# Retention and a Swish MLP in one program: wider transfers for half of w_in, its up projections in groups of four, and later scores for the first two tails

## The chip, the cores and the metric

The kernel runs on one core of one Trainium2 chip. The metric is device time in microseconds (us). A core has TensorE (PE; its weight loads are listed apart as PEld), VectorE (DVE), ScalarE (ACT), GpSimd (POOL) and SyncE (SP), which issues nearly all transfers of this kernel. PE writes into PSUM, here eight banks of 128 x 512 f32 values; DVE and ACT copy from there into the on-chip memory SBUF.

## What is computed

Retention over 8 batches, 8 heads, 576 positions and 64 values a head, and behind it an MLP with a Swish whose beta differs by column:

```python
scores = scale * np.matmul(q, k.transpose(0, 1, 3, 2))
Dmat = np.where(rel >= 0, gamma[:, None, None] ** rel[None, :, :], 0.0)
attn_out = np.matmul(scores * Dmat, v)
x = attn_out.transpose(0, 2, 1, 3).reshape(B * S, H * D)    # 4608 x 512
h = x @ w_in                                                # w_in: 512 x 2048
g = h * (1.0 / (1.0 + np.exp(-beta * h)))
out = g @ w_out                                             # w_out: 2048 x 512
```

## The kernel before

**Tiles.** Of each batch's 576 positions, 512 are four chunks of 128 (`seq` entries 0 to 31); the last 64 positions are its tail. Two batches' tails make one chunk of 128, so there are four tails (entries 32 to 35). The MLP works on blocks of 512 rows: block m is batch m's chunks, and block 8 is the four tails together. The blocks' order is 0 to 6, 8, 7 (L49).

**MLP.** For a block, `up` (L480) makes one of 16 tiles of 128 columns of h by four matmuls of 128x512 (one for each `ko`, a quarter of the 512 inputs) into a PSUM bank; ACT takes the Swish of it into `gT`. `down` (L514) adds four matmuls at a time into an accumulator `po`; after 16 it is copied to `ot` and sent out. Block 0's first six tiles of h are made in pairs by `up_pair` (L493): u = 0 does the first two `ko` of both, u = 1 the last two.

**Weights.** `pieces` (L165) cuts w_in into eight pieces of 256 columns. `load_w_in` (L171) brings a piece in with rows of 1 KB, the first three pieces in two halves by `ko`; two pieces share one tile `wt`, of which there are four. `cast_w_in` (L180) makes bf16 of it, four casts of 128x256 for a piece, even `ko` on POOL and odd on DVE. `load_w_out` (L189) reuses the `wt` tiles, in rows of 2 KB, and `cast_w_out` (L195) scales and casts. All loads of w_in are issued before the first matmul of the program, w_out's in the list below, and behind these the loads of the next batches.

**Retention.** For a batch, POOL (DVE at first) scales q and casts k (`kn`, L288), v is scaled (`vn`, L268); PE or, from batch 2 on, a transposing transfer (L296) turns them. A tail takes six loads (L108), POOL's preparation `pre` (L276 to L278) and one transposing transfer, `x_tail`. `first(i)` (L654) makes the scores of entries i and i + 1 (`a_sc`, L328): 8 matmuls each into two banks, the even entry's with the tag "sc" and the odd one's with "O"; DVE multiplies them with the causal mask into `R`. `tails(i)` (L674) makes the outputs of two tails (`a_O4` L442, `a_cross4` L459) in the two "O" banks, which `x4` (L470) copies, one by ACT and one by DVE. A tail's tile `tln` shares the tag "qn", of two buffers, with the tiles of q.

**Order.** The kernel writes its order out by hand. `fill` is a list of PE's large units (one `up`, or four matmuls of `down`: 0.86 us each). Streams of other steps have positions in that list; `merged` (L541) runs a step ahead of the first unit whose number is not below its position, and steps of equal position in the order of their streams. So each engine, SP's queue too, does its part in this order. `base[n]` is the number of the first unit of the n-th block. The tails hang on block 6: with its first unit as 0, the loop at L703 puts `first` of batch 7's chunks at 3 and 10, of tails 32 and 33 at 17, and of tails 34 and 35 at 24; `tails` comes 5 later. `pair_prep` (L680) puts the loads, preparations and transposes at fixed distances ahead of `first`. Around the first two tails the list before is, with numbers counted from block 6's first unit:

```
-14 load_tail(0)  -4.5 pre(32)  -4 load_tail(1)  -3 x_k(7, 1)  -3 load_tail(2)
4 pre(33)  4 load_tail(3)  5 x_tail(32)  6.5 pre(34)  7.5 x_tail(33)
12 pre(35)  12 x_tail(34)  14.5 x_tail(35)  15 outputs(28)
17 first(32)  22 tails(32)  24 first(34)  29 tails(34)  32 up(8, 0)
```

PSUM's eight banks are three of tag "mm" (`ph`, `po`), two "O", two "sc" and one "st".

Of the kernel before, what the change touches and what calls it, by code (L numbers as in the profile page):

```python
# [11 lines left out]
F32 = mybir.dt.float32  # L12
# [7 lines left out]
def kernel(  # L20
# [11 lines left out]
    B, H, S, D = q.shape  # L32
    d_model = H * D
    d_ff = moe_w_in.shape[1]
    N = B * S
    P = 128
    HP = H // 2
    KO = d_model // P
    FO = d_ff // P
    MB = 512  # L40
# [21 lines left out]
    psum = ctx.enter_context(tc.psum_pool(name="psum", bufs=1))  # L62
# [68 lines left out]
    for h in range(H):  # L131
# [15 lines left out]
                            fill=0.0, base=0, channel_multiplier=-1)  # L147
# [14 lines left out]
    tiny = consts.tile([P, FO], F32, name="tiny")  # L162
    WG = 4

    pieces = [(f, 256) for f in range(0, d_ff, 256)]  # L165
    NP = len(pieces)
    w_in_r = moe_w_in.rearrange("(ko ki) f -> ki ko f", ki=P)
    w_out_r = moe_w_out.rearrange("(fo fi) n -> fi fo n", fi=P)
    wts, whole = {}, [None]

    def load_w_in(g):  # L171
        f0, fn = pieces[g]
        if f0 % 512 == 0:
            whole[0] = stage.tile([P, KO, 512], F32, name="wt", tag="wt", bufs=4)
        t = whole[0][:, :, f0 % 512:f0 % 512 + fn]
        for w in (slice(0, 2), slice(2, KO)) if g < 3 else (slice(0, KO),):
            nc.sync.dma_start(t[:, w], w_in_r[:, w, f0:f0 + fn])  # L177
        wts[g] = t

    def cast_w_in(g, kos=range(KO)):  # L180
        t = wts[g]
        f0, fn = pieces[g]
        for ko in kos:
            if ko % 2 == 0:
                nc.gpsimd.tensor_copy(w_in_sb[:, ko, f0:f0 + fn], t[:, ko])  # L185
                continue
            nc.vector.tensor_copy(w_in_sb[:, ko, f0:f0 + fn], t[:, ko])  # L187
# [16 lines left out]
    for g in range(NP):  # L204
        load_w_in(g)
# [284 lines left out]

    phs = {}

    def up_pair(m, fo, u):  # L493

        if m not in gts:
            gts[m] = sb.tile([P, FO, CB, P], BF16, name="gT", tag="gT", bufs=2)
        fs = (fo, fo + 1)
        if u == 0:
            tag = ("mm", "O", "sc")[fo // 2]
            for f in fs:  # L500
                phs[f] = psum.tile([P, MB], F32, name="ph", tag=tag, bufs=3 if tag == "mm" else 2)
        for ko, f in [(ko, f) for ko in (2 * u, 2 * u + 1) for f in fs]:
            nc.tensor.matmul(phs[f][:], w_in_sb[:, ko, f * P:(f + 1) * P], xts[m][:, ko],
                             start=(ko == 0), stop=(ko == KO - 1))
            if ko == KO - 1:
                nc.scalar.activation(gts[m][:, f], phs[f][:], ACT.Silu, scale=beta_sb[:, f:f + 1])
# [44 lines left out]
    def F(f, *a):  # L551
        return lambda: f(*a)
# [5 lines left out]
    for n in range(4):  # L558
# [34 lines left out]
    a_cross(3, True)  # L593
    a_O(3)
    cast_w_in(0, (0, 1))
    a_x(3)
    cast_w_in(0, (2, 3))
    a_st(3)
    cast_w_in(1)
    nc.vector.reciprocal(rbeta_sb[:], beta_sb[:])  # L600

    nc.gpsimd.memset(causal2[:], 1.0)
    nc.gpsimd.affine_select(out=causal2[:], in_=causal2[:], pattern=[[1, P]], compare_op=ALU.is_ge,
                            fill=0.0, base=0, channel_multiplier=-1)
    nc.gpsimd.memset(causal2[:TL, TL:], 0.0)

    fill = [F(up_pair, 0, fo, u) for fo in (0, 2, 4) for u in range(2)] + [F(up, 0, fo) for fo in range(6, FO)]
    d0 = len(fill)
    def down_rows(n):

# [69 lines left out]
    def pair_prep(i, at):  # L680
        b, c = seq[i]
        if b is None:
            if c:
                return [(at - 27, F(load_tail, c)), (at - 20, F(load_tail, c + 1)), (at - 17.5, F(pre, i)),
                        (at - 12, F(pre, i + 1)), (at - 12, F(x_tail, i)), (at - 9.5, F(x_tail, i + 1))]
            return [(at - 31, F(load_tail, c)), (at - 21.5, F(pre, i)), (at - 21, F(load_tail, c + 1)),
                    (at - 13, F(pre, i + 1)), (at - 12, F(x_tail, i)), (at - 9.5, F(x_tail, i + 1))]
        n, st = full.index(i), []
        if b == XB:
            if c == 0:  # L690
                return [(d0 + 13, F(pre, i + x, (0,))) for x in range(2)] + \
                       [(d0 + 14, F(pre, i + x, (1,))) for x in range(2)]
            return [(u1 + 8 + x / 2, F(pre, i + x)) for x in range(2)]
        if c == 0:
            st += [(at - 30, F(load_q, b, (0,)))] + ([(at - 30, F(x_k, XB, 1))] if b == XB + 1 else [])
            st += [(at - 30, F(load_q, b, (1,)))] + [(at - 20 + x, F(pre_q, b, x)) for x in range(4)]
            st += [(at - 14 + 1.5 * x, F(x_q, b, x)) for x in range(2)]
        early = b == XB + 1 and c > 0
        return st + [(at - (25.4 if early else 28), F(load_kv, n)), (at - (25.3 if early else 26), F(load_kv, n + 1)), (at - 16, F(pre, i)),
                     (at - 15, F(pre, i + 1)), (at - (13 if c else 11.5), F(x_k, b, c // 2))]  # L700

    todo = list(range(2 * CB, len(seq), 2))
    for n in range(1, B - 1):  # L703

        take = [i for i in todo if seq[i][0] == n + 1 or n == B - 2]
        todo = todo[len(take):]
        lo, hi = (base[n] + 17, base[n + 1] - 9.5) if n == 1 else (base[n] + 3, base[n + 1] - 8)
        at = [lo + x * (hi - lo) / (len(take) - 1) for x in range(len(take))]
        if len(take) == 2 and n > 1:
            at[1] -= 6  # L710
        for i, t in zip(take, at):
            st = pair_prep(i, t) + [(t, F(first, i))]
            if seq[i][0] is None:
                st.append((t + 5, F(tails, i)))
            elif seq[i][1] > 0:
                st.append((t + 5, F(outputs, i - 2)))
            streams.append(st)
# [32 lines left out]
```

## Time and profile before

| What | Value |
|---|---|
| Median of three runs | 304.92 us (304.61 to 305.0) |
| The profiled execution | 304.39 us |
| Its span (first to last instruction) | 302.7 us |
| PE busy in the span | 296.1 us |
| ACT / POOL / DVE busy | 133.8 / 108.2 / 103.8 us |
| 128x512 matmuls of up (L487) and of down (L521) | 592 and 608, the costliest groups of PE |
| Granted PE clock | 1.0 all the way |

The span is what the profile covers; 1.7 us of the execution's time lies around it. A line of a timeline gives start and length in us, engine, line of the kernel, operation, what is written and read, how many instructions were merged and, in brackets, the idle time of the engine before it and who ended that. SPq is SP issuing transfers. In the table of stretches, each engine has its busy us and its number of instructions in brackets; PE's clock, the share of the 16 DMA engines and GB/s follow.

### The profile page before, as it was taken

To read this page: it belongs to the slowest core of one execution; us is meant where nothing else is said; L and a number is where in the kernel's file an instruction comes from. 1 tells how busy PE (TensorE), PEld (TensorE's weight loads), DVE (VectorE), ACT (ScalarE), POOL (GpSimd) and SP (SyncE) were. 2 spreads that over 40 slices of the span, in tenths; PEclk is the share of its full clock that TensorE was granted. 3 is DMA by queue.
4 is the path that set the end of the run, shared out by engine and by line. 5 is a ranking of instruction groups with operands and counts; after the bars stand their busy time and mean duration, and the time that the engine had idled before them with its cause. 6 is when DMAs were issued, how large, how long until landed. Compare 5 with 4: busy or idle time off the path is not lost.

```text
span 302.7 us, 5782 instructions
## 1 busy us (share of the span) xinstructions
PE 296.1 (98%) x2345; PEld 151.5 (50%) x2345; DVE 103.8 (34%) x192; ACT 133.8 (44%) x227; POOL 108.2 (36%) x212
## 2 busy tenths in 40 slices
PE   8799999999999999999999999999999999999996
PEld 5554455855544454445444544454454444444444
DVE  6554556604640443043222413151346510020012
ACT  5577446781247223732274227521761058107700
POOL 3666007673942733551355043960452000000000
PEclk9999999999999999999999999999999999999999
DMA  8999999999999999909991899997996100131011
GB/s 212 220 346 364 383 253 241 221 193 241 180 243 272 254 199 225 260 13 167 248 244 37 158 229 248 212 184 186 193 196 108 70 36 0 36 70 35 2 69 69
DMA packets 129290, 53.86 MB, mean 178 GB/s; under 512 B 110048, under 2 KB 122736, under 8 KB 129264
## 3 DMA queue, kind: packets, MB, share of 16 engines
q1 hardware_dynamic: 129232, 53.49, 80.0%
q8 instruction: 18, 0.29, 0.4%
q14 instruction: 8, 0.07, 0.1%
q10 hardware_dynamic: 32, 0.01, 0.0%
HBM read 36.71 MB, written 9.44 MB: 152 GB/s over the span
## 4 chain that ended last, share of the span: by engine, by line
PE 84%; DMA 8%; SPq 5%; POOL 1%; issue 0%; DVE 0%
PE po L521 38%; PE ph L487 37%; DMA kvn<-in_k_dram 3%; SPq L94 3%; PE sc L338 3%; DMA wt<-in_moe_w_out_dram 3%; PE O L455 2%; DMA wt<-in_moe_w_in_dram 2%; PE st L413 2%; PE O L467 1%; SPq L82 1%; SPq L177 1%; POOL w_in_sb L185 0%; PE O L386 0%; PE T L318 0%
## 5 line engine op out<-in xcount | busy, mean ns | idle before, releaser
L489 ACT ACTIVATE gT<-ph,beta_sb 128x512 bf16<-128x512 f32 (+1 forms) x148 | 97.0, 659 | 80.8 <-PE ph L487 80.6
L521 PE MATMUL po<-w_out_sb,gT 128*128 128x512 bf16 (+2 forms) x608 | 129.1, 368 | 0.0
L487 PE MATMUL ph<-xT,w_in_sb 128*128 128x512 bf16 (+1 forms) x592 | 122.8, 365 | 0.0
L521 PEld LDWEIGHTS <-gT 128*128 128x128 bf16 x608 | 56.9, 98 | 63.4
L487 PEld LDWEIGHTS <-w_in_sb 128*128 128x128 bf16 x592 | 56.8, 98 | 60.7 <-POOL w_in_sb L185 0.7
L343 DVE TENSOR_TENSOR R<-sc,causal 128x512 bf16<-128x512 f32 x72 | 45.0, 684 | 79.1 <-PE sc L338 79.0
L528 DVE COPY ot<-po 128x512 f32<-128x512 f32 (+2 forms) x34 | 22.4, 658 | 77.2 <-PE po L521 77.2
L288 POOL CAST kn<-kvn 128x128 bf16<-128x128 f32 (+2 forms) x80 | 25.8, 357 | 59.7 <-DMA kvn<-in_k_dram 59.3
L268 POOL TENSOR_TENSOR vn<-kvn,gv 128x512 bf16<-128x512 f32 x32 | 33.3, 1042 | 8.7 <-DMA kvn<-in_v_dram 4.8
L257 POOL TENSOR_TENSOR qs<-qn,gq 128x256 bf16<-128x256 f32 (+1 forms) x36 | 26.3, 758 | 27.6 <-DMA qn<-in_q_dram 27.6
L421 ACT CAST sbq<-st 128x256 bf16<-128x256 f32 x18 | 6.7, 371 | 35.8 <-PE st L413 35.8
L475 DVE CAST xT<-O 128x512 bf16<-128x512 f32 x20 | 12.7, 685 | 20.9 <-PE O L467 20.9
L338 PE MATMUL sc<-qT,kT 64*128 64x128 bf16 x256 | 10.8, 218 | 0.6 <-ACT kT L319 0.6
L338 PEld LDWEIGHTS <-kT 64*128 64x128 bf16 x288 | 8.2, 94 | 5.5 <-issue 3.8
L475 ACT CAST xT<-O 128x512 bf16<-128x512 f32 x8 | 4.7, 589 | 13.4 <-PE O L467 13.4
L276 POOL TENSOR_TENSOR kn<-tln,gq 128x128 bf16<-128x128 f32 (+1 forms) x12 | 5.6, 470 | 13.6 <-DMA tln<-in_q_dram 7.1
L185 POOL CAST w_in_sb<-wt 128x256 bf16<-128x256 f32 x16 | 7.2, 472 | 5.4 <-DMA wt<-in_moe_w_in_dram 5.2
L210 PE MATMUL ph<-warm 128*128 128x128 f32 (+1 forms) x24 | 7.3, 444 | 1.2 <-DVE warm L119 1.2
L455 PE MATMUL O<-R,vn 128*64 128x128 bf16 x224 | 7.7, 220 | 0.0
L187 DVE CAST w_in_sb<-wt 128x256 bf16<-128x256 f32 x16 | 5.3, 360 | 6.6 <-DMA wt<-in_moe_w_in_dram 6.6
L413 PEld LDWEIGHTS <-kn 128*64 128x64 bf16 x192 | 4.8, 111 | 5.5 <-issue 4.2
L202 DVE TENSOR_SCALAR w_out_sb<-wt,rbeta_sb 128x512 bf16<-128x512 f32 x13 | 5.9, 484 | 4.8 <-DMA wt<-in_moe_w_out_dram 4.8
(71 smaller groups left out, 112.8 us busy)
## 6 DMA issues: line engine op xcount, KB each, us to landing
qn<-in_q_dram SPq DMA_DIRECT2D x16, 512.0 KB, 5.4
kvn<-in_k_dram SPq DMA_DIRECT2D x32, 256.0 KB, 5.4
kvn<-in_v_dram SPq DMA_DIRECT2D x32, 256.0 KB, 5.1
out_dram<-ot SPq DMA_DIRECT2D x31, 256.0 KB, 2.9
wt<-in_moe_w_out_dram SPq DMA_DIRECT2D x8, 512.0 KB, 8.9
wt<-in_moe_w_in_dram SPq DMA_DIRECT2D x5, 512.0 KB, 8.6
wt<-in_moe_w_in_dram SPq DMA_DIRECT2D x6, 256.0 KB, 5.9
out_dram<-ot SPq DMA_DIRECT2D x9, 128.0 KB, 2.3
```

The source lines that it names most:

```text
L257: nc.gpsimd.tensor_tensor(batch[b]["qs"][:, cs, to], q_tiles[b][:, hs, cs].rearrange("p h i d -> p i h d"), gq[:, cs, hs].unsqueeze(3).to_ ...
L268: nc.gpsimd.tensor_tensor(live[i]["vn"][:], kv_tiles.pop(i)[:, 1], gains(gv, c), ALU.mult)
L288: nc.gpsimd.tensor_copy(kn[:, c % 2, to], t[:, 0, hs])
L338: nc.tensor.matmul(view(sc[j][:, p, :]), L["kT"][r, p, :], rhs, start=True, stop=True, skip_group_check=True)
L343: nc.vector.tensor_tensor(R[:, j], sc[j][:], m_b, ALU.mult)
L413: nc.tensor.matmul(st[j * D:(j + 1) * D, p, :], L["kn"][:, 2 * p + j, :], L["vn"][:, head_of(b, p, j), :], start=(c == 0 and p == 0), stop ...
L455: nc.tensor.matmul(out4(i, p, h % 2), L["vn"][:, h, :], rhs if b is None else rhs.rearrange("k (i s) -> k i s", i=CB), start=c % 2 == 0 an ...
L475: (nc.scalar.copy if n == 1 else nc.vector.tensor_copy)(to, O.rearrange("k p i s -> k p (i s)") if b is None else O[:])
L487: nc.tensor.matmul(ph, w_in_sb[:, ko, fo * P:(fo + 1) * P], xts[m][:, ko, :, w], start=(ko == 0), stop=(ko == KO - 1))
L489: nc.scalar.activation(gts[m][:, fo, :, w], ph, ACT.Silu, scale=beta_sb[:, fo:fo + 1])
L521: nc.tensor.matmul(po[:, :nn], gT[:, fo, ms, :], w_out_sb[:, fo, n0:n0 + nn], start=(fo == 0), stop=(fo == FO - 1))
L528: (nc.scalar.copy if m == 0 else nc.vector.tensor_copy)(ot, po[:, :nn])
```

## The change

The second half of w_in (columns 1024 to 2047) is cut otherwise: two stretches of 512 columns, each in two pieces by rows (`ko` 0 and 1, then 2 and 3), so its transfers have rows of 2 KB and its casts are 128x512, two for a piece. There are still eight pieces and eleven transfers. `up_pair` becomes `ups`, which takes any number of tiles and the banks' tags. Block 0's tiles 0 to 7 are made as before; tiles 8 to 11 and 12 to 15 in groups of four, first the two lower `ko` of all four, then the upper two of one tile after the other. The groups take banks of "O" and "sc", and of "mm" and "st". Empty places in the list keep its length, so all other positions stay.

In the loop at L703, the third entry of the last round (tails 32 and 33) goes 1.5 units later, and with it its loads, preparations, transposes and outputs; the fourth (tails 34 and 35) stays.

```diff
-    pieces = [(f, 256) for f in range(0, d_ff, 256)]
+    low_rows, high_rows = slice(0, KO // 2), slice(KO // 2, KO)
+    pieces = [(f, 256, (low_rows, high_rows) if f < 768 else (slice(0, KO),)) for f in range(0, d_ff // 2, 256)]
+    pieces += [(f, 512, (w,)) for f in range(d_ff // 2, d_ff, 512) for w in (low_rows, high_rows)]
...
-        for w in (slice(0, 2), slice(2, KO)) if g < 3 else (slice(0, KO),):
+        for w in rows:
             nc.sync.dma_start(t[:, w], w_in_r[:, w, f0:f0 + fn])
...
-        for ko in kos:
+        for ko in kos or range(rows[0].start, rows[-1].stop):
...
-    def up_pair(m, fo, u):
+    def ups(m, fs, u, banks):
...
-            tag = ("mm", "O", "sc")[fo // 2]
-            for f in fs:
-                phs[f] = psum.tile([P, MB], F32, name="ph", tag=tag, bufs=3 if tag == "mm" else 2)
-        for ko, f in [(ko, f) for ko in (2 * u, 2 * u + 1) for f in fs]:
+            for f, tag in zip(fs, banks):
+                phs[f] = psum.tile([P, MB], F32, name="ph", tag=tag, bufs=dict(mm=3, O=2, sc=2, st=1)[tag])
+        kos = (2 * u, 2 * u + 1)
+        for ko, f in [(ko, f) for ko in kos for f in fs] if u == 0 or len(fs) == 2 else [(ko, f) for f in fs for ko in kos]:
...
-    fill = [F(up_pair, 0, fo, u) for fo in (0, 2, 4) for u in range(2)] + [F(up, 0, fo) for fo in range(6, FO)]
+    fill = [F(ups, 0, (fo, fo + 1), u, tags) for fo, tags in ((0, ("mm", "mm")), (2, ("O", "O")), (4, ("sc", "sc"))) for u in range(2)]
+    fill += [F(up, 0, fo) for fo in (6, 7)]
+    for fo, tags in ((8, ("O", "O", "sc", "sc")), (12, ("mm", "mm", "mm", "st"))):
+        for u in range(2):
+            fill += [F(ups, 0, range(fo, fo + 4), u, tags), lambda: None]
...
+        if n == B - 2:
+            at[2] += 1.5
```

More of the change, by code (lines that the diff above doesn't have):

```diff
@@ L171, in load_w_in, with cast_w_in @@
     def load_w_in(g):
-        f0, fn = pieces[g]
-        if f0 % 512 == 0:
+        f0, fn, rows = pieces[g]
+        if f0 % 512 == 0 and rows[0].start == 0:
             whole[0] = stage.tile([P, KO, 512], F32, name="wt", tag="wt", bufs=4)
         t = whole[0][:, :, f0 % 512:f0 % 512 + fn]
-        for w in (slice(0, 2), slice(2, KO)) if g < 3 else (slice(0, KO),):
+        for w in rows:
             nc.sync.dma_start(t[:, w], w_in_r[:, w, f0:f0 + fn])
         wts[g] = t
-    def cast_w_in(g, kos=range(KO)):
+    def cast_w_in(g, kos=None):
         t = wts[g]
-        f0, fn = pieces[g]
-        for ko in kos:
+        f0, fn, rows = pieces[g]
+        for ko in kos or range(rows[0].start, rows[-1].stop):
             if ko % 2 == 0:
@@ L491 @@
     phs = {}
-    def up_pair(m, fo, u):
+    def ups(m, fs, u, banks):
         if m not in gts:
             gts[m] = sb.tile([P, FO, CB, P], BF16, name="gT", tag="gT", bufs=2)
-        fs = (fo, fo + 1)
         if u == 0:
-            tag = ("mm", "O", "sc")[fo // 2]
-            for f in fs:
-                phs[f] = psum.tile([P, MB], F32, name="ph", tag=tag, bufs=3 if tag == "mm" else 2)
-        for ko, f in [(ko, f) for ko in (2 * u, 2 * u + 1) for f in fs]:
+            for f, tag in zip(fs, banks):
+                phs[f] = psum.tile([P, MB], F32, name="ph", tag=tag, bufs=dict(mm=3, O=2, sc=2, st=1)[tag])
+        kos = (2 * u, 2 * u + 1)
+        for ko, f in [(ko, f) for ko in kos for f in fs] if u == 0 or len(fs) == 2 else [(ko, f) for f in fs for ko in kos]:
             nc.tensor.matmul(phs[f][:], w_in_sb[:, ko, f * P:(f + 1) * P], xts[m][:, ko],
```

## The prediction

> **What bounds the kernel now.** I read the page first. TensorE (PE) is busy 296.1 us of the 302.7 us span, and the chain that ended last is 84% PE. That is PE being full, so a change pays only where PE waits, or where it makes PE wait. Next I read the PE timeline in order of time: it stands without a break from 24.4 us to the end, but for a few small places. The waits of 40 to 47 us name who was late there, and the table of stretches (third fence) has PE 3.63 of 3.70 us busy:
>
> ```profile
> PE 296.1 (98%) x2345; PEld 151.5 (50%) x2345; DVE 103.8 (34%) x192; ACT 133.8 (44%) x227; POOL 108.2 (36%) x212
> ```
> ```profile
> PEld L318 <- POOL kn L288: 0.6, 2, 0.3
> PEld L312 <- DVE qs L260: 0.2, 1, 0.2
> ```
> ```profile
> 42.90:46.60 3.70, 3.63 (x36) 2.10 (x35) 2.12 (x4) 2.08 (x3) 1.30 (x2) 1.00 0.80 172
> ```
>
> The reader sees that PE waits here for batch 1's q (through VectorE, DVE, qs) and batch 1's first k (through POOL, kn). Comparing starts of neighbouring matmuls with the usual distance of their form, I find 0.16 us lost inside the transposes at 44.27 and 0.24 us before the one at 45.12: 0.39 us (unrounded 0.156 and 0.237). All other gaps from 45 us on are the 0.09 to 0.12 us that PE loses wherever a 128*128 matmul follows a smaller tile form or the reverse.
>
> Both producers wait for transfers, so the third view is DVE's timeline over the weights. With it I read how fast pieces land:
>
> ```profile
> 24.87 0.69 DVE L187 CAST w_in_sb<-wt 128x256 bf16<-128x256 f32 x2 [0.82 <-DMA wt<-in_moe_w_in_dram]
> 26.38 0.70 DVE L187 CAST w_in_sb<-wt 128x256 bf16<-128x256 f32 x2 [0.81 <-DMA wt<-in_moe_w_in_dram]
> 27.88 0.70 DVE L187 CAST w_in_sb<-wt 128x256 bf16<-128x256 f32 x2 [0.81 <-DMA wt<-in_moe_w_in_dram]
> 29.37 0.70 DVE L187 CAST w_in_sb<-wt 128x256 bf16<-128x256 f32 x2 [0.79 <-DMA wt<-in_moe_w_in_dram]
> ...
> 38.86 0.88 DVE L202 TENSOR_SCALAR w_out_sb<-wt,rbeta_sb 128x512 bf16<-128x512 f32 x2 [0.89 <-DMA wt<-in_moe_w_out_dram]
> 40.23 0.49 DVE L202 TENSOR_SCALAR w_out_sb<-wt,rbeta_sb 128x512 bf16<-128x512 f32 x1 [0.49 <-DMA wt<-in_moe_w_out_dram]
> ```
>
> Each starts as its 512 KB lands: every 1.50 us for w_in (rows of 1 KB), every 1.37 us in these two of w_out (rows of 2 KB); over all eight from 30.80 to 40.23 it is 9.43/7 = 1.35 us. The DMA row of the page is at 9 tenths through this stretch.
>
> Last, the tails: in the timelines of PE, of DVE and of the queue of SP (which issues the transfers):
>
> ```profile
> 226.94 1.03 PE L521 MATMUL po<-w_out_sb,gT 128*128 128x512 bf16 x4
> 227.90 0.66 PE L338 MATMUL sc<-kT 64*128 64x128 bf16 x16
> 228.49 4.49 PE L521 MATMUL po<-w_out_sb,gT 128*128 128x512 bf16 x20
> 232.91 0.64 PE L455 MATMUL O<-R,vn 128*64 128x128 bf16 x16
> 233.48 0.46 PE L467 MATMUL O<-kT,end 64*64 64x64 bf16 x32
> 233.87 1.90 PE L521 MATMUL po<-w_out_sb,gT 128*128 128x512 bf16 x8
> 235.70 0.62 PE L338 MATMUL sc<-kT 64*128 64x128 bf16 x16
> ```
> ```profile
> 233.98 0.69 DVE L475 CAST xT<-O 128x512 bf16<-128x512 f32 x1 [1.99 <-PE O L467]
> ```
> ```profile
> 218.13 1.33 SPq L108 DMA_DIRECT2D tln<-in_q_dram  x2
> 219.51 2.07 SPq L108 DMA_DIRECT2D tln<-in_k_dram  x2
> 221.63 1.31 SPq L108 DMA_DIRECT2D tln<-in_v_dram  x2
> 223.04 6.17 SPq L296 DMA_TRANSPOSE kT<-kn  x4
> ```
>
> PE waits nowhere here. Between the first tails (end 233.87) and the next scores (235.70) stand eight matmuls, and in that time DVE and ScalarE (ACT) empty the two O banks.
>
> **Part 1, w_in's second half.** Bytes and number of issues stay (six of 256 KB, five of 512 KB). Four transfers get rows of 2 KB instead of 1 KB; by the two rates each lands 1.505 - 1.355 = 0.15 us sooner, 0.6 us after four. Everything queued behind them (w_out, q1, batch 1's k and v) moves up by that, since SP issues without a break from 31.27 to 46.30 and what it issues waits its turn (the first k 10.4 us in the chain of waits). Casts: 16 of 128x256 become 8 of 128x512. POOL's 128x512 cast of f32 takes 0.61 to 0.68 us (the kn row at 45.54 and 44.38) against 0.92 for the two it replaces; DVE's 128x512 from SBUF about 0.5 (w_out rows, 0.48). They are beside PE: the first wide piece lands at about 24.7, POOL is done by 25.4, and up 8 starts at 32.60 - 32 x 0.216 = 25.69, so 0.3 us of cover; if it went, PE would wait by what is over. Later pieces have more. The 0.22 us that PE loses at 21.8 and 23.7 stays: those pieces are unchanged and ahead in the queue.
>
> A page of the Trainium skill speaks against so large an effect: "DMA: Bandwidth & Descriptors", section "Why small descriptors are slow", gives about 3 cycles of overhead per packet beside one cycle per 32 bytes. My estimate from it is 70 cycles for two rows of 1 KB and 67 for one of 2 KB, so 0.065 us a piece and 0.26 us in all, where the trace shows 0.15 a piece. The sum goes by the trace.
>
> PE's 0.39 us: qs, ready 0.6 us sooner, no longer delays the transposes, and kn, ready at 44.5 instead of 45.07, is there before PE would want it at 44.73. So **-0.39**. What is late next after that is nothing before 68 us: transposed keys land 0.8 us or more before their scores at 68.7 and 74.8, and their loads also move up.
>
> **Part 2, groups of four.** The same 40 matmuls at 0.216 us. Two groups hold four PSUM banks each; those of O and sc were emptied by 25.2, when ACT ended the last pair's swish (23.87 + 1.27), and the third bank is first wanted at 26.1; the st bank has been idle since 19.5. In the second half of a group the swish results come every 0.43 us and ACT takes 0.58 a piece, so the last ends near 34.0 instead of 33.5. The down projection's second accumulator wants a bank at 32.82 that is free at about 32.80 to 32.86. I take **0**, at most 0.05. The empty places in the list issue nothing.
>
> **Part 3, the tails.** With unit u = 0.864 us, the list's position 0 at 209.81: scores of the first two tails go from 17 to 18.5, hence ahead of unit 19 instead of 17; their outputs from 22 to 23.5, ahead of unit 24. There stand already the scores of the last two tails, unmoved. So outputs and next scores become neighbours. Those scores write "sc" for the third tail and both "O" banks for the fourth, and these hold the first tails' outputs until x4 has copied them. In before's times: last output matmul at 233.74; scores of the third tail from 233.87, eight in 0.30, so the fourth's would start at 234.16; DVE's copy ends at 233.98 + 0.69 = 234.67, plus 0.06 as seen from kn to PE at 45.12. PE stands still **+0.57**; behind it are the remaining down units, so the end moves with it. Removed are two changes of form (0.12 and 0.10 us, around 233.87 and 235.70), added is one (about 0.10): **-0.12**.
>
> Moved as well: six loads each of the first and second tail, two POOL preparations and two transposes. First tail's loads (194 us) have 7 us of room. The second's now stand behind the key transpose at 211.95 and the third's loads: by SP's rows (transposes 1.30, six loads 4.0) they start at about 213.0 instead of 207.82; q lands 3.2 us after issue, POOL starts at 217.0, and its vn is done at about 221.1 instead of 216.0. The fourth's loads at position 4 need a buffer of two: its preparation of the second tail now stands at 5.5, so SP, in order, waits until 221.1 where it had issued at 218.13. Behind SP's wait stand the transposes of all four tails. The fourth's loads took 4.8 us at 218.13 and 4.0 elsewhere: first transpose at 225.2 to 226.0, second 1.4 later; that one landed 3.3 us after issue, so at 229.9 to 230.8. PE wants the second tail's scores at 227.90 + 1.73 + 0.30 = 229.93. Cost 0 to 0.85; I take **+0.2**, nearest to the 4.0 us that three of the four tails' loads needed.
>
> **Sum.** -0.39 + 0 + 0.57 - 0.12 + 0.2 = +0.26 us. The profiled execution took 304.39 us (span 302.7 and 1.7 around it), so 304.65; the median shown is 304.92, 0.53 higher, hence **305.2 us**, no change that a measurement of this kernel tells (0.2%, 0.6 us).
>
> **Rivals.**
> - Forecast: 40%.
> - The tail waits don't appear (scheduling leaves units between, or the copies are quicker): 304.92 - 0.39 - 0.12 = 304.4. For: the slack of PE's queue is read from modelled ends. Against: both O banks are needed, by name. 18%.
> - Smaller gain in the head: only half of the 0.6 us reaches batch 1's k (DMA's share in the third fence is 0.80, so the queue there is not held by bytes alone). Then kn is ready at 45.07 - 0.3 = 44.77, PE starts on it 0.05 later, at 44.82 instead of 44.73, and 0.09 of the 0.39 stays: 305.3. The even pitch of landings before it speaks against. 7%. The skill's page, with its 0.26 us, would give this case.
> - SP's chain at its long end (0.85 instead of 0.2): 305.8. 15%.
> - **Slower by one mechanism:** the fourth tail's load gets the third tail's buffer rather than the second's. It then waits for the third preparation, done at 221.1 + 3.3 = 224.4 (POOL's row from 219.49 to 222.76), transposes follow 4.1 us later, the second lands at 233.2 and PE waits 3.3 us: 304.92 - 0.39 + 0.45 + 3.3 = 308.3. It decides once SP's load issues after about 222 us. Nothing in before shows the choice; the second's buffer is freed first. 10%.
> - Part 1 does not do what it says (PE's gap at 44 to 45 stays): 304.92 + 0.65 = 305.6. Against: rows show w_out's rate. 10%.
>
> Below 304.4 lies half of the second case, above 306.2 the slot case: range **304.4 to 306.2**. Faster by over 0.2% (below 304.3): 0.08, from the second case and a bit of the first. Slower (above 305.5): 0.32, from the slot (0.10), the long chain (0.12), no head gain (0.05) and the forecast's edge (0.05). Same: 0.60.
>
> **What would show it.** w_in's wide casts 1.35 us apart and qs starting near 41.1; no PE wait at 44 to 45; scores and outputs of tails adjacent near 235 us with PE idle some 0.6 us inside the second set of scores; SP's fourth load issuing near 221 and PE's wait at the first tails' scores under 0.9 us. A wait of 3 us there, or none in the second scores, would prove me wrong.

## The result and the profile after

The changed kernel takes 312.21 us (median of six, 311.81 to 313.81) against 304.96 us, a ratio of 1.0249 (95% interval 1.0225 to 1.0274): slower by 7.25 us. The forecast was 305.2 us, no change. The profiled executions stand further apart, 312.78 and 304.39 us, with spans of 311.1 and 302.7 us; terms below are theirs.

First the page: PE's total and its granted clock in 40 slices (of 7.8 us).

```profile
PE 295.6 (95%) x2311; PEld 152.5 (49%) x2345; DVE 102.8 (33%) x188; ACT 133.1 (43%) x227; POOL 107.5 (35%) x208
PEclk9999999999999999999999999999995999999999
```

PE is busy as long as before, in a longer span, and one slice, the 31st, has half the clock. Two rows of the table of stretches show the head and this slice (busy us and number of instructions of PE, PEld, DVE, ACT, POOL, then clock, DMA share, GB/s):

```profile
42.90:46.60 3.70, 3.70 (x43) 2.43 (x41) 1.84 (x3) 2.44 (x5) 1.64 (x3) 1.00 1.01 209
235.50:241.50 6.00, 6.00 (x18) 2.25 (x17) 2.08 (x4) 0.00 (x0) 0.00 (x0) 0.56 0.34 88
```

The wait at 44 us is gone (PE is busy 3.70 of 3.70 us). The tails stand in PE's timeline:

```profile
226.57 2.75 PE L522 MATMUL po<-w_out_sb,gT 128*128 128x512 bf16 x12
233.79 0.51 PE L340 MATMUL sc<-kT 64*128 64x128 bf16 x8 [4.46 <-DMA kT<-kn]
234.96 0.61 PE L340 MATMUL sc<-kT 64*128 64x128 bf16 x8 [0.67 <-DMA kT<-kn]
235.50 7.07 PE L522 MATMUL po<-w_out_sb,gT 128*128 128x512 bf16 x19
...
243.46 0.40 PE L340 MATMUL sc<-kT 64*128 64x128 bf16 x8
244.27 0.43 PE L340 MATMUL sc<-kT 64*128 64x128 bf16 x8 [0.41 <-ACT xT L477]
```

PE stands 4.5 and then 0.7 us for the transposes of the first two tails. The 20 matmuls behind them (one record is missing in the line) take from 235.50 to 242.50, 7.00 us, where the same twenty took 232.91 - 228.49 = 4.42. The last line is the wait for the O banks. Why the transposes are late stands in SP's queue and in POOL's timeline. First two lines of SP's queue before, then the queue after, then POOL after:

```profile
194.19 1.76 SPq L108 DMA_DIRECT2D tln<-in_q_dram  x2
...
198.88 0.58 SPq L534 DMA_DIRECT2D out_dram<-ot  x1
```
```profile
198.21 0.36 SPq L535 DMA_DIRECT2D out_dram<-ot  x1
198.61 1.43 SPq L108 DMA_DIRECT2D tln<-in_q_dram  x2
...
214.88 1.27 SPq L108 DMA_DIRECT2D tln<-in_q_dram  x2
...
225.44 1.28 SPq L108 DMA_DIRECT2D tln<-in_q_dram  x2
...
230.06 5.52 SPq L298 DMA_TRANSPOSE kT<-kn  x4
```
```profile
222.83 0.40 POOL L279 CAST kn<-tln 128x256 bf16<-128x256 f32 x1 [2.23 <-DMA tln<-in_k_dram]
...
224.37 1.04 POOL L280 TENSOR_TENSOR vn<-tln,gv 128x512 bf16<-128x512 f32 x1
```

The first tail's loads now stand behind an output that SP can issue only at 198.21, when DVE has copied PE's accumulator (before, they went ahead of it, at 194.19). The second's start at 214.88 (before 207.82, ahead of the third's). The fourth's start at 225.44, at once when POOL has read the second's buffer (224.37 + 1.04 = 225.41), and all four transposes come behind them, at 230.06 instead of 223.04.

Between the down units ahead of the first tails' scores and block 8's first up lie 252.61 - 226.57 = 26.04 us, before 244.23 - 226.94 = 17.29: 8.75 more. Of these, by the starts: 4.5 before the first scores (233.79 instead of 229.26), 0.9 between first and second, 2.6 in the twenty slow matmuls and 0.2 in the second scores at the same clock, 0.6 for the O banks (0.81 between the two sets of eight, instead of 0.24); the changes of form take some 0.1 off. The head gives 0.37 back (batch 7's scores at 211.96 instead of 212.33), and the spans differ by 8.4.

### The profile page after: what moved, and what is told of

It reads as the page before. It is cut to its first block, busy times and chain, and to the rows that moved or that the text cites. A ratio compares the mean times of both kernels' runs of the same rounds, so it can differ in the third digit from the quotient of the medians.

```text
span 311.1 us, 5740 instructions
## 1 busy us (share of the span) xinstructions
PE 295.6 (95%) x2311; PEld 152.5 (49%) x2345; DVE 102.8 (33%) x188; ACT 133.1 (43%) x227; POOL 107.5 (35%) x208
## 4 chain that ended last, share of the span: by engine, by line
PE 80%; SPq 7%; DMA 6%; issue 2%; POOL 2%; DVE 1%; ACT 1%; DVEq 0%; POOLq 0%
PE po L522 36%; PE ph L489 32%; PE ph L504 4%; SPq L108 4%; DMA tln<-in_k_dram 3%; PE sc L340 3%; SPq L94 2%; DMA kvn<-in_k_dram 2%; PE O L457 2%; PE st L415 1%; DMA kT<-kn 1%; SPq L298 1%; PE O L469 1%; POOL vn L280 1%; DVE R L345 1%
## 5 line engine op out<-in xcount | busy, mean ns | idle before, releaser
L491 ACT ACTIVATE gT<-ph,beta_sb 128x512 bf16<-128x512 f32 (+1 forms) x140 | 91.4, 657 | 79.4 <-PE ph L489 79.0
L489 PE MATMUL ph<-xT,w_in_sb 128*128 128x512 bf16 (+1 forms) x546 | 114.5, 364 | 0.7 <-issue 0.2
L489 PEld LDWEIGHTS <-w_in_sb 128*128 128x128 bf16 x560 | 53.8, 98 | 56.6 <-POOL w_in_sb L187 0.4
L504 PE MATMUL ph<-xT,w_in_sb 128*128 128x512 bf16 x54 | 12.3, 379 | 0.3 <-ACT xT L398 0.2
L507 ACT ACTIVATE gT<-ph,beta_sb 128x512 bf16<-128x512 f32 x14 | 8.6, 685 | 4.2 <-PE ph L504 4.2
L504 PEld LDWEIGHTS <-w_in_sb 128*128 128x128 bf16 x56 | 5.4, 97 | 6.7 <-POOL w_in_sb L187 0.4
L187 POOL CAST w_in_sb<-wt 128x256 bf16<-128x256 f32 (+1 forms) x12 | 7.0, 594 | 4.7 <-DMA wt<-in_moe_w_in_dram 4.6
```

Source lines behind the costliest of these rows:

```text
L489: nc.tensor.matmul(ph, w_in_sb[:, ko, fo * P:(fo + 1) * P], xts[m][:, ko, :, w], start=(ko == 0), stop=(ko == KO - 1))
L491: nc.scalar.activation(gts[m][:, fo, :, w], ph, ACT.Silu, scale=beta_sb[:, fo:fo + 1])
```

## The experiments

The theory after the result (A in the expectations) was: the loss is made by the tails' loads in SP's queue, and a lower clock behind PE's idle time adds to it. Against it stood: the head costs (H), the later place of scores and outputs costs (S), and the clock falls for a reason of its own.

**Parts 1 and 2 alone.** The changed kernel without

```diff
-        if n == B - 2:
-            at[2] += 1.5
```

> Parts 1 and 2 alone, tails as before. Theory A (the loss is made by the tails' loads in SP's queue): 304.96 - 0.37 = 304.6 us, no wait of PE at 44 to 45 us, clock 1.0. Rival H (the head costs time or clock later on): well above 305.5. Rival S (the later place of scores and outputs costs): 304.6 too.

Measured: 304.53 us against 304.97, ratio 0.9985 (0.9971 to 0.9999). The head gains what was forecast, so H falls. Its profile shows one thing more, in PE's timeline:

```profile
227.66 0.43 PE L340 MATMUL sc<-kT 64*128 64x128 bf16 x8
228.61 0.40 PE L340 MATMUL sc<-kT 64*128 64x128 bf16 x8 [0.51 <-DMA kT<-kn]
```

With the old order the second tail's transpose is already the next thing late: it landed at 228.56 here, and in the kernel before at 227.75, 0.4 us ahead of its scores.

**Part 3 alone** (the two lines above, added to the kernel before).

> Part 3 alone on the kernel before. A and S: 312.2 + 0.37 = 312.6 us, with PE idle 5 to 6 us ahead of the first tails' scores and a lower clock behind it. H: about 305.

Measured: 312.02 us, ratio 1.0258 (1.0226 to 1.029); PE idles 4.69 and 0.48 us ahead of the first tails' scores, and its clock is at half from within this idle time to 238.66 us. Part 3 is the whole loss.

**Scores and outputs later, preparation not.**

```diff
-        if n == B - 2:
-            at[2] += 1.5
...
+            late = 1.5 if seq[i] == (None, 0) else 0
-            st = pair_prep(i, t) + [(t, F(first, i))]
+            st = pair_prep(i, t) + [(t + late, F(first, i))]
...
-                st.append((t + 5, F(tails, i)))
+                st.append((t + late + 5, F(tails, i)))
```

> The changed kernel with scores and outputs of the first two tails 1.5 units later, but their loads, preparations and transposes where they were. A: no wait at the first tails' scores, 0.57 us of wait for the O banks at the last tails' scores less 0.12 us for changes of form: 304.6 + 0.45 = 305.05 us. S: near 312.

Measured: 304.84 us, ratio 1.0003 (0.9992 to 1.0015). S falls: the new place itself costs only the wait for the O banks, read again in PE's timeline as eight scores that start 0.80 us behind the first eight instead of 0.24:

```profile
235.52 0.40 PE L340 MATMUL sc<-kT 64*128 64x128 bf16 x8
236.32 0.43 PE L340 MATMUL sc<-kT 64*128 64x128 bf16 x8 [0.41 <-ACT xT L477]
```

**Preparation later, scores and outputs not** (the same with `pair_prep(i, t + late)` and `t` in the other two places).

> The changed kernel with only loads, preparations and transposes 1.5 units later, scores and outputs where they were before. A: the transposes land as late, and two down units that stood ahead of the wait are behind it: 312.2 + 1.73 - 0.45 = 313.5 us. S: 304.6.

Measured: 313.25 us, ratio 1.0279 (1.0251 to 1.0306), with 5.80 us of idle time at the first scores. So the loss is made by loads, preparations and transposes. That the median is 1.0 us above the changed kernel's says little: the four executions stand at 312.28 and 312.50 us (mean granted clock 0.989, as in most of the changed kernel's) and at 313.99 and 314.11 (clock 0.984).

**The idle time filled.**

```diff
-            st = pair_prep(i, t) + [(t, F(first, i))]
+            st = pair_prep(i, t) + ([(t, F(warm_up, 10))] if seq[i] == (None, 0) else []) + [(t, F(first, i))]
```

> The changed kernel with ten f32 matmuls of 128x256 on zeros (0.43 us each, 4.3 us, results unused) directly ahead of the first tails' scores, where PE idles 4.5 us. Theory C (PE's clock is cut in half behind the idle time because of it): the stretch of 5 us at 0.56 clock goes, 312.2 - 2.6 = 309.6 us. Rival (the clock falls for another reason, as the stretch's own work): 312.2 us.

Measured: 310.18 us, ratio 1.0194 (1.0151 to 1.0237), by the medians 2.0 us less than the changed kernel, though one of the four executions took 312.76. The clock is 1.0 in all four. In PE's timeline the filling work (two records for each of its ten matmuls) ends where the transposes land, and the matmuls behind run at their usual 0.22 us:

```profile
228.97 4.48 PE L212 MATMUL ph<-warm 128*128 128x256 f32 x20
233.56 0.40 PE L340 MATMUL sc<-kT 64*128 64x128 bf16 x8
235.37 4.26 PE L522 MATMUL po<-w_out_sb,gT 128*128 128x512 bf16 x19 [0.16 <-issue]
```

The low clock is made by the idle time. It is worth some 2 us of the loss by these medians, and 2.6 by the twenty matmuls of the changed kernel's profile.

**The first tail's loads back ahead of the output.**

```diff
-            return [(at - 31, F(load_tail, c)), (at - 21.5, F(pre, i)), (at - 21, F(load_tail, c + 1)),
+            return [(at - 32.5, F(load_tail, c)), (at - 21.5, F(pre, i)), (at - 21, F(load_tail, c + 1)),
```

> The changed kernel with the first tail's six loads back ahead of the output that waits for PE (position -14 instead of -12.5), all else shifted. If the three changes in SP's queue add up: the second tail's loads start 2.3 us sooner, the fourth's about as much, PE's idle time of 5.5 us falls to about 3: 309 us or, if the clock then holds, 307. If the buffer wait alone decides: 312.

Measured: 308.20 us, ratio 1.0111 (1.0082 to 1.0139). The fourth's loads issue at 223.00, 2.4 us sooner. In the profile PE waits 1.67 and 0.70 us and the clock holds; of the four executions, two have a clock of 1.0 (307.36 and 307.66 us) and two one of 0.994 (308.73 and 309.0). So undoing this one move past an output takes some 4 us of the 7 away.

**The second tail's loads back ahead of the third's** (`at - 22.5` for `at - 21`).

> The changed kernel with the second tail's loads back at position -4, ahead of the key transpose and of the third tail's loads. Its preparation ends near 218.5, so the fourth's loads, though they still wait for its buffer by the list, issue by about 219 and PE finds the transposes landed at 228.5 where it wants them at 229.3: 305.1 us. If the first tail's loads alone decide: about 310.

Measured: 306.71 us, ratio 1.0064 (1.0041 to 1.0087). The buffer wait is gone: the second's preparation ends at 218.90, and the fourth's loads issue at 221.70, when SP comes to them. But PE still waits, which I had not expected:

```profile
230.67 0.40 PE L340 MATMUL sc<-kT 64*128 64x128 bf16 x8 [0.65 <-DMA kT<-kn]
231.91 0.40 PE L340 MATMUL sc<-kT 64*128 64x128 bf16 x8 [0.84 <-DMA kT<-kn]
```

SP's queue, 2.7 us later than I had reckoned at the fourth's loads and with the first tail's loads still behind the output, issues the first transpose only at 225.83, and the two land 4.8 and 4.6 us after issue, where they took 3.7 and 3.3 before. This move alone takes 5.5 us of the 7 away. The savings of the separate moves are not terms to be added, since each shortens the same chain.

**The fourth tail's loads behind the first two transposes** (`at - 14.9` for `at - 20`).

> The changed kernel with the fourth tail's loads placed behind the transposes of the first two tails (position 9.1 instead of 4). A: nothing of the first two tails stands behind the buffer wait, so PE's 5.5 us ahead of their scores go; the fourth's own transpose is late by up to 1.7 us: 305 to 307 us. If the transposes are late by their own preparation: no gain, 312.

Measured: 305.79 us, ratio 1.0066 (1.0027 to 1.0105). The median hides two groups: four executions with a clock of 0.999 or 1.0 took 305.35 to 305.79 us, three with 0.994 took 308.08 to 309.02. The profile is of one of the latter (308.08). In it the first transpose issues at 221.40, and PE's wait there shrinks to 0.30 us; the fourth's own is late by 1.88, a little more than expected. In the stretch behind, the clock is at half again:

```profile
237.95 0.61 PE L340 MATMUL sc<-kT 64*128 64x128 bf16 x8 [1.88 <-DMA kT<-kn]
239.00:240.00 1.00, 1.00 (x3) 0.35 (x3) 0.88 (x2) 0.00 (x0) 0.00 (x0) 0.50 0.00 0
```

**Scores and outputs one unit later** (as above with `late = 1`).

> Parts 1 and 2, with the first two tails' scores and outputs one unit later (18 and 23) and their loads, preparations and transposes where they were. The second tail's transpose, 0.5 us late for PE in the profile of parts 1 and 2 alone, is then covered, and one unit (0.86 us) stays between outputs and the next scores, more than the 0.57 us of the copies: 304.5 less up to 0.5, 304.1 us. If that wait is only in the one profile, or is replaced by the copies': 304.5.

Measured: 305.27 us, ratio 1.0014 (1.0004 to 1.0023), and so not what was expected. The copies do fit into one unit (no wait at the last tails' scores), but the second tail's transpose landed at 230.04, 5.2 us after issue, where with parts 1 and 2 alone it took 3.5 and landed at 228.56:

```profile
230.08 0.40 PE L340 MATMUL sc<-kT 64*128 64x128 bf16 x8 [1.17 <-DMA kT<-kn]
```

What went with it is in the last section.

**All four tails' scores and outputs 1.5 units later** (`late = 1.5 if seq[i][0] is None else 0`).

> Parts 1 and 2, with scores and outputs of all four tails 1.5 units later and all loads, preparations and transposes where they were. Outputs and the next scores are then two units apart as before: the wait for the O banks goes and two changes of form come back, 304.84 - 0.57 + 0.12 = 304.4 us. If the wait for the O banks costs nothing at the end: 304.8 or more.

Measured: 304.30 us, ratio 0.9986 (0.9977 to 0.9996), 0.54 us under the version in which outputs and next scores are neighbours. That confirms the wait for the O banks at the end of the kernel too. Against the kernel before it is no better than parts 1 and 2 alone (ratios 0.9986 and 0.9985).

**The head's parts apart.** Wide transfers with plain ups, tails as before:

```diff
-    for fo, tags in ((8, ("O", "O", "sc", "sc")), (12, ("mm", "mm", "mm", "st"))):
-        for u in range(2):
-            fill += [F(ups, 0, range(fo, fo + 4), u, tags), lambda: None]
+    fill += [F(up, 0, fo) for fo in range(8, FO)]
```

> Part 1 without part 2: the wide transfers, tiles 8 to 15 one after the other, tails as before. Tile 8 wants its third quarter at 26.1 us and the cast of the second wide piece ends at about 26.9: PE waits 0.8 us there, and keeps the gain at 44 us: 304.5 + 0.8 = 305.3 us. If groups and plain order are alike: 304.5.

Measured: 305.34 us, ratio 1.0021 (1.0012 to 1.0029), 0.8 us over both parts together. The wait is where it was expected, but smaller: PE's matmuls are 0.71 us apart at 26.24 instead of 0.22, a loss of 0.5 and not of 0.8. And groups of four on narrow pieces (`pieces` all of 256 columns, tails as before):

> Part 2 without part 1: groups of four on pieces of 256 columns, tails as before. Tile 10's first matmul wants the second piece at 26.1 us and its cast ends at about 26.9: 0.8 us of wait at the first group, of which the 0.39 us at 44 us are got back because PE comes there later: 304.97 + 0.4 = 305.4 us. If the groups alone make the gain: 304.5.

Measured: 304.84 us, ratio 1.0004 (0.9995 to 1.0012). PE stands 0.8 us at 26.1 as expected, and comes to batch 1's first scores at 46.94 instead of 46.54; yet the medians show no loss. The profiles do: block 8's first up starts at 244.63 instead of 244.23, and the spans are 303.1 and 302.7 us. The 0.4 us are not won back between the two profiled executions, but that of the kernel before (304.39 us) lies 0.5 under its median of 304.88, and that of the groups alone (304.80) lies at its own. What the other executions of the kernel before lose is not shown. The two parts need each other for the gain.

## Why the prediction was wrong, point by point

- **Head, -0.39 us: right.** The wide pieces' casts stand 1.35 us apart, as w_out's rows had said:

```profile
24.66 0.43 DVE L189 CAST w_in_sb<-wt 128x512 bf16<-128x512 f32 x1 [0.67 <-DMA wt<-in_moe_w_in_dram]
...
28.72 0.43 DVE L189 CAST w_in_sb<-wt 128x512 bf16<-128x512 f32 x1 [0.92 <-DMA wt<-in_moe_w_in_dram]
```

  The gain is 0.37 us at batch 7's scores and 0.44 in the medians. The Trainium skill's page "DMA: Bandwidth & Descriptors", section "Why small descriptors are slow (HBM only)", would have given 0.07 a piece, by the estimate from its 3 cycles per packet; the trace has 0.15, and the trace decides. One size was off with no harm: POOL's wide cast takes 0.87 us, not 0.61 to 0.68, so the cover ahead of up 8 was 0.2 us and not 0.3.
- **Groups of four, 0: right**, given the wide transfers.
- **O banks, +0.57: right in mechanism and size**: 0.57 by the starts in the changed kernel (0.81 less the usual 0.24), 0.54 between the versions with and without neighbours. The changes of form (-0.12) were not measured by themselves.
- **The step that failed: the SP chain, "+0.2, at most 0.85".** The order was right, with the buffer that was expected (the fourth's loads at 225.44, behind the second's preparation at 225.41; the rival with the third's buffer did not happen). Two numbers in it were wrong. First, "First tail's loads (194 us) have 7 us of room": I checked when their data are needed, not what they were moved past. At position -12.5 they stand behind an output that waits for PE. Before, SP had issued them while that output was not ready; now SP stands idle there and spends 4.8 us on the loads (198.61 to 203.41) behind the wait, and the second's loads start 2.3 us later than worked out (214.88, against 213.0 less the head's 0.37). Putting them back gave 4 us. Second, the sum took "q lands 3.2 us after issue" and, behind it, a preparation as quick as before's: q took 4.1 and 4.2, and k's second half 5.8, for which POOL waited 2.23 us instead of 0.88. The preparation ended at 225.4 instead of 221.1, the first transpose issued 4 to 5 us late, and PE lost 5.4 us there (4.5 and 0.9 by the starts) instead of 0.2.
- **The term that was missing: the clock.** A wait of PE was priced at its own length. At 4.5 us it also cost 2 to 2.6 us at half clock; with part 3 alone, where more of the half clock fell into the idle time, the twenty matmuls lost 1.3. The Trainium skill states such a rule ("TensorE: Matmul & The Clock Gate", section "Part 1: The HAM clock gate (the "warmup" mystery)"): half the clock after an idle window of about 3.4 us, back after a busy one. The trace of the changed kernel agrees for its long wait. With the fourth's loads moved, less than such a window of idle time was enough (1.88 of 3.41 us, last section), and there the measurement decides.

## What to carry to other kernels

A step moved in a hand-written order moves all that it issues, on every queue: walk each in-order queue with the new order and look for what the moved issues now stand behind (a wait for another engine above all), not only for the time at which their data are needed. Of a transfer that a chain hangs on, take the longest landing that the trace shows nearby, not the median. And price a stall of the engine that bounds the kernel with the clock that it can lose.

## What the runs showed of the hardware that I had not expected

- The record of the granted clock is at 0.5 for 6.83 us in the changed kernel, in part 3 alone and in the late preparation, and for 3.41 us with the fourth's loads moved: two steps and one step of 3.41. Continue these steps backwards, and add up PE's idle time in each (by the timeline, whose matmul ends are modelled). The clock fell at the end of steps with 3.27 (changed kernel), 3.08 (late preparation), 2.19 (part 3 alone) and 1.88 us (fourth's loads moved) of idle time, and held after steps with 1.58 (first tail's loads put back) and 1.20 us (changed kernel, the step before). So in these traces the limit lies at about half a step, and the same wait can cost a step or none, by where it lies in the steps. At half clock a step in which PE has work throughout costs half of it, 1.7 us. That is also the distance between executions: the changed kernel took 311.81 to 312.78 us with a mean clock of 0.989 and 313.81 with 0.984, which is one step more.
- The late landings go with an instruction fetch. In the packets of the trace a packet of 16 KB on the instruction queue takes 0.9 to 1.6 us. With parts 1 and 2 alone it comes at 229.5 us, behind the second tail's transpose; in all three versions with only scores and outputs later it comes at 227.7 to 228.0, and some 256-byte packets beside it take up to 1.4 or 1.5 us, where the median is 0.02; there the second tail's transpose landed 5.1 to 5.2 us after issue. Another, at 219.3 in the changed kernel, goes with the 5.8 us of k. That the fetch is the cause was not tried by itself.
